# Setting unit 5 in a written order on all engines, with a table that places the six last conversions of w_out

## The chip, the core and the metric

The kernel runs on one core of one Trainium2 chip. The metric is the device time of one execution in microseconds (us). The engines are named as in the profile: PE (TensorE matmul), PEld (its weight load), DVE (VectorE), ACT (ScalarE), POOL (GpSimd), SP (SyncE, which issues most loads); "ACTq" and "SPq" are the sequencers of ACT and SP when they issue a DMA.

## The reference

Attention with a decaying state (8 heads, 4 batches, 768 positions, head size 64), then a feed-forward layer with a gate.

```python
for t in range(S):
    state = gamma[None, :, None, None] * state + np.einsum('bhd,bhe->bhde', k[:, :, t], v[:, :, t])
    y[:, :, t] = scale * np.einsum('bhd,bhde->bhe', q[:, :, t], state)
...
h = x @ w_in                       # 3072 x 512 by 512 x 2048
relu6 = np.clip(h + 3.0, 0.0, 6.0)
g = h * relu6 / 6.0
return (g @ w_out).astype(np.float32)   # 2048 x 512
```

The weights arrive as 64-bit floats.

## The kernel before, in words

**Tokens** are cut into 24 rows of 128 and 6 units of 512 (four rows each). A **tile of h** is 128 of the 2048 hidden columns by the 512 tokens of a unit, 16 tiles for a unit, 96 in all. Each is 12 matmuls of 128x128 by 128x512 (`products`, L431): both operands are split into a high and a low part, and three of the four products are taken for each of the four blocks of 128. `finish` then does the gate: `relu` on ACT (L438), `to_memory` (a DMA on the ACT queue, L465, that writes the tile *before* this one to the scratch tensor `gd`), and `times` on DVE (L442). Four PSUM buffers hold tiles of h.

**The first stage** (`head`) runs attention and units 0 and 1 in an order that is written out by hand. **`steady`** follows, a loop over `steps`: n = 0..15 are the tiles of unit 2, 16..31 of unit 3, 32..47 of unit 4, 48..63 of unit 5. At n = 1, 5, ... 45 it also does the attention of a row (`chunk_burst`): matmuls into `uz`, `sc` and `y`, ACT copies of the state out of `uz` (`keep`, L388), one DVE product (`weigh`, L352) and the split of the new x (L196, L199).

**Conversion of w_out.** It comes in 16 pieces (n_w2 = 0..15, two to each of eight tiles `w2c[j]`). One piece is `w2_steps`: a fetch into `st` (two buffers, 4 KB a partition each, issued on SP by `read`, L136), then steps with one letter each: `a` and `b` (DVE, L160, L164, bits of exponent and mantissa), `e` (ACT, L169), `q` and `f` (DVE, L172, L177, `f` being the last reader of `st`), `w` (DVE, L183), `1 2 3 0` (four DVE subtractions of 128x128, L116), `g` and `h` (ACT, L196, high parts), `k` and `l` (DVE, L199, low parts; `l` is the last reader of the buffer `ws`). The buffers `we`, `wb`, `ww` and `ws` exist once each. Pieces 0 to 9 are done in `steady`, four tiles of h for each piece, in the order `abqe`, `fw1`, `g230`, `hkl`.

**Who sets the order.** `head` and `steady` are under `manual_schedule` for PE, DVE, ACT and SP: their instructions keep the order in which the code names them. What is written outside goes through a planner that simulates the program, keeps a priority for each instruction, and may put an instruction between those of a set order. In the kernel before, `steady` ends at n = 47. Unit 5 is written outside it: PE alone has a set order there, and the planner places the gates of unit 5 and the conversions 10 to 15 (`build_w2`, called at tiles 4, 6, 8, 10, 12 and 14 of unit 5) on DVE, ACT and SP.

**The output stage** (L698) multiplies `gd` by `w2c` for three blocks of 1024 tokens, in four groups for each block, and each group in four rounds c = 0..3. A round loads `gd` into `gv` (two DMAs on SP, L668 in the first group), forms a sum on DVE (L119 in the first group), and splits two operands into `gc` (high part on ACT, L196; low part on DVE, L199). The first operand is split from `gv`, the second from the sum, which is kept in `spare`, a tile that takes over a slot of w_in after the last matmul that reads it. A round is 24 matmuls. The loads and sums of round 0 have high priority; the later DVE work of the first group is tied behind `end`, the last `times`:

```python
if sb == 0 and g == 0 and c == 0:
    first.enter_context(tc.high_priority())
elif sb == 0 and g == 0:
    first.enter_context(tc.issue_after(end))
```

`gv` rotates over three places: round 0 uses the pool `late` (in space that attention held), round 1 the pool `gv0`, round 2 the pool `gv1`, round 3 `late` again. `gv0` and `gv1` are laid over the space of the first stage, from its start, 8 KB a partition each; the pool that starts there is `wst`, with `st`, `we`, `wb`, `ww` and `ws` (16 KB in all).

Of the kernel before, what the change touches and what calls it, by code (L numbers as in the profile page):

```python
# [10 lines left out]
F32R = mybir.dt.float32r  # L11
# [9 lines left out]
P = 128  # L21
# [9 lines left out]
def retention_ffn(ctx: ExitStack, tc: tile.TileContext, qkv, w_in, w_out, dkc, dqc, dmc, tab, out, B, H, S, D):  # L31
# [8 lines left out]
    NF = w_in.shape[0]  # L40
# [3 lines left out]
    NROW = NT // P  # L44
    ROWS_B = S // P
    UR = 4
    UT = UR * P
    NU = NROW // UR
# [4 lines left out]
    FIRST = 3 * UR + 1  # L53
# [23 lines left out]
    BLK = 2 * P  # L77
    SLOT = 14 * BLK
    NSLOT = 10
    WHEN = (4, 6, 8, 10, 12, 14)  # L80
    STEADY = (NU - 1 - 2) * NF
    BUILT = 10
    PIECES = ("g230", "hkl", "abqe", "fw1")


    const = ctx.enter_context(tc.tile_pool(name="const", bufs=1))
    dram = ctx.enter_context(tc.tile_pool(name="dram", bufs=1, space=DRAM))
# [24 lines left out]
    def nm(s):  # L112
        return f"{s}_{next(serial)}"

    def dve_sub(out_, a, b):
        return nc.vector.tensor_tensor(out=out_, in0=a, in1=b, op=ALU.subtract)  # L116
# [29 lines left out]
    def fetch(src):  # L146
        st = wst.tile([P, src.shape[-1]], I64, tag="st", name=nm("st"), bufs=2)
        read(st, src)
        return st

    def conversion(st):

        n = st.shape[-1]
        words = st.bitcast(I32).rearrange("p (n w) -> p n w", w=2)
        lo, hi = words[:, :, 0], words[:, :, 1]
        t = {}

        def a():
            t["e"] = wst.tile([P, n], I32, tag="we", name=nm("we"))
            nc.vector.tensor_scalar(out=t["e"], in0=hi, scalar1=0x7FF00000, scalar2=None, op0=ALU.bitwise_and)  # L160

        def b():
            t["b"] = wst.tile([P, n], I32, tag="wb", name=nm("wb"))
            nc.vector.tensor_scalar(  # L164
                out=t["b"], in0=hi, scalar1=0xFFFFF, scalar2=0x100000, op0=ALU.bitwise_and, op1=ALU.bitwise_or
            )

        def e():
            nc.scalar.activation(out=t["e"], in_=t["e"], func=AF.Relu, scale=8.0, bias=ebias)  # L169

        def q():
            nc.vector.scalar_tensor_tensor(  # L172
                out=t["b"].bitcast(F32), in0=lo.bitcast(U32), scalar=2.0**-32, in1=t["b"], op0=ALU.mult, op1=ALU.add
            )

        def f():
            nc.vector.scalar_tensor_tensor(  # L177
                out=t["e"], in0=hi, scalar=-2147483648, in1=t["e"], op0=ALU.bitwise_and, op1=ALU.bitwise_or
            )

        def w():
            t["w"] = wst.tile([P, n], F32, tag="ww", name=nm("ww"))
            nc.vector.scalar_tensor_tensor(  # L183
                out=t["w"], in0=t["b"].bitcast(F32), scalar=2.0**-20, in1=t["e"].bitcast(F32), op0=ALU.mult, op1=ALU.mult
            )
            return t["w"]

        return {"a": a, "b": b, "e": e, "q": q, "f": f, "w": w}
# [6 lines left out]
    def high(hi, src):  # L195
        nc.scalar.activation(out=hi, in_=src, func=AF.Copy)  # L196

    def low(lo, hi, src):
        nc.vector.tensor_tensor(out=lo, in0=src, in1=hi, op=ALU.subtract)  # L199
# [8 lines left out]
    def place(shape, dtype, name, own):  # L208

        return wpool.tile(shape, dtype, tag="w0" if own else "w", name=name, bufs=1 if own else NSLOT - 1)  # L210
# [17 lines left out]
    w2c = {}  # L228

    def w2_steps(n, st):  # L230

        j, h = divmod(n, 2)
        if not h:
            w2c[j] = place([P, 7, 2, 2, P], F32R, nm("w2"), j == 5)
        made = conversion(st)
        to, t = w2c[j], {}

        def w():
            t["w"] = made["w"]().rearrange("p (b n) -> p b n", b=4)
            t["s"] = wst.tile([P, 4, P], F32, tag="ws", name=nm("ws"))  # L240

        def sub(o, a, b):
            block = lambda i: t["s"][:, i] if i < 4 else t["w"][:, i - 4]
            return lambda: dve_sub(block(o), block(a), block(b))

        steps = made | {
            "w": w,
            "1": sub(1, 4, 5),
            "2": sub(2, 7, 1),
            "3": sub(3, 7, 4),  # L250
            "0": sub(0, 2, 6),
            "g": lambda: high(to[:, 0:3, 0, h], t["w"][:, 1:4]),
            "h": lambda: high(to[:, 3:7, 0, h], t["s"]),
            "k": lambda: low(to[:, 0:3, 1, h], to[:, 0:3, 0, h], t["w"][:, 1:4]),
            "l": lambda: low(to[:, 3:7, 1, h], to[:, 3:7, 0, h], t["s"]),
        }
        return steps

    def build_w2(n):
        steps = w2_steps(n, fetch(w_out[divmod(n, 2)]))  # L260
        for k in "abeqfw1230gkhl":
            steps[k]()


    bits = place([TROWS, tab.shape[1]], I32, "bits", True)
    nc.scalar.dma_start(out=bits, in_=tab)
# [179 lines left out]
    def tile_of_h(u, jj):  # L446

        h = ps_h.tile([P, UT], F32, tag="h", name=nm("h"))
        for k in range(NK):
            products(h, u, jj, k)  # L450
        return u, jj, h

    def finish(u, jj, h):

        g, after = relu(h)
        to_memory(after)
        return times(u, jj, g, h)
# [103 lines left out]
    steps = [(u, jj) for u in range(2, NU) for jj in range(NF)]  # L561

    def steady():

        fetched, build, pending = [fetch(w_out[0, 0])], None, []
        load(FIRST)
        for n, step in enumerate(steps[:STEADY]):
            pending.append(tile_of_h(*step))
            for tile_ in pending[:-1]:
                finish(*tile_)  # L570
            del pending[:-1]
            b, row = (n - 2) // UR, FIRST + n // UR
            if n % UR == 2 and b < BUILT:
                build = w2_steps(b, fetched[b])
                if b + 1 < BUILT:
                    fetched.append(fetch(w_out[divmod(b + 1, 2)]))
            for k in PIECES[n % UR] if 0 <= b < BUILT else "":
                build[k]()
            if n % UR == 1:
                finish(*pending.pop())  # L580
                chunk_burst(row)
                if row + 1 < NROW:
                    load(row + 1)
        for tile_ in pending:
            finish(*tile_)

    engines = mybir.EngineType
    with tc.manual_schedule(engines={engines.PE, engines.DVE, engines.Activation, engines.SP}):
        head()
        steady()  # L590
    order = ExitStack()
    order.enter_context(tc.manual_schedule(engines={mybir.EngineType.PE}))

    att.close()
    late = ctx.enter_context(tc.tile_pool(name="late", bufs=1, side="right", reuse_waits="tile"))
    n_w2 = BUILT
    for u, jj in steps[STEADY:]:
        if jj in WHEN:
            build_w2(n_w2)
            n_w2 += 1  # L600
        end = finish(*tile_of_h(u, jj))
    to_memory(end)
    ph1.close()

# [43 lines left out]
    for sb in range(NT // TB):  # L648
        for g, ids in enumerate(GROUPS):
# [7 lines left out]
            for c in range(NFP // CP):  # L657
                with ExitStack() as first:
# [5 lines left out]
                    for jj in range(CP):  # L664
                        j = c * CP + jj
# [8 lines left out]
                    a, b = gv[:, 0], gv[:, 1]  # L674
                    s = sums[c]
# [17 lines left out]
                for i, gc in zip(ids, ops):  # L693
                    for h in range(2):
                        for jj in range(CP):
                            j = c * CP + jj
# [22 lines left out]
            else:  # L719
                for k, i, m in (("s", 2, 0), ("v", 3, 1)):  # L720
# [3 lines left out]
                    else:  # L724
                        for h in range(2):
                            for n in range(2 if (i, h) == (3, 1) else 1):
                                to = slice(n * BLK, (n + 1) * BLK) if (i, h) == (3, 1) else slice(0, UT)
# [88 lines left out]
```

## Time and profile before

| | |
|---|---|
| median of 3 runs | 579.49 us (578.61 to 583.13) |
| the profiled execution's own time | 581.04 us |
| its span, first to last instruction | 579.3 us |
| mean granted TensorE clock | 0.994 |
| PE busy | 565.8 us, 98% |
| DVE busy | 423.8 us, 73% |
| ACT busy | 247.1 us, 43% |
| POOL busy | 45.4 us, 8% |

A row of a timeline has the start in us, the duration in us, the engine, the line, the operation with output and input, the count, and in brackets the idle time just before with what ended it. A row of the chain of waits has start, length and what it was. A row of the stretches has, for each engine, busy time and in brackets the count, then the granted clock and the DMA share.

### The profile page before, as it was taken

What the parts mean: (1) busy time and instruction counts of PE and PEld (TensorE: products, weight loads), DVE (VectorE), ACT (ScalarE), POOL (GpSimd) and SP (SyncE); (2) the same over time, 40 slices, a digit from 0 to 9 for tenths busy, and PEclk for the clock granted to TensorE, in tenths of its full rate; (3) what the DMA queues carried; (4) which work ended last, traced back from release to release, by engine and by line L of the source; (5) the groups of instructions that cost most, each with busy time, mean ns of one, the idle gap of its engine ahead of it and who ended that gap; (6) DMA issues with size and microseconds to landing.
All of it is one profiled execution on the core that took longest, in us unless ns stands there. A gap on an engine that the chain in (4) does not pass through costs nothing.

```text
span 579.3 us, 12415 instructions
## 1 busy us (share of the span) xinstructions
PE 565.8 (98%) x5126; PEld 463.5 (80%) x5126; DVE 423.8 (73%) x588; ACT 247.1 (43%) x368; POOL 45.4 (8%) x51
## 2 busy tenths in 40 slices
PE   7799999999999999999999999999999999999997
PEld 5677887888888888888788888888888888888885
DVE  5489998733677678777726989679776698866871
ACT  3285544432444444434324555543434343344430
POOL 3201011121111111112000000000000000000000
PEclk9799999999999999999999999999999999999999
DMA  8866777835665666666542576465754757636611
GB/s 267 289 212 218 251 250 241 272 132 182 208 212 204 209 218 222 232 221 233 204 158 92 180 246 226 149 216 164 272 180 115 247 148 258 214 107 189 213 74 72
DMA packets 58324, 115.82 MB, mean 200 GB/s; under 512 B 5782, under 2 KB 6678, under 8 KB 58268
## 3 DMA queue, kind: packets, MB, share of 16 engines
q1 hardware_dynamic: 44144, 89.67, 48.1%
q10 hardware_dynamic: 14124, 25.37, 11.6%
q8 instruction: 40, 0.66, 0.5%
q14 instruction: 16, 0.13, 0.1%
HBM read 83.56 MB, written 31.46 MB: 199 GB/s over the span
## 4 chain that ended last, share of the span: by engine, by line
PE 92%; DMA 5%; issue 1%; DVE 1%; SPq 0%; POOL 0%; DVEq 0%
PE h L431 44%; PE o L698 40%; PE y L384 3%; PE sc L384 3%; PE uz L384 3%; DMA early<-in_qkv 2%; DMA st<-in_w_in 2%; DMA qt<-in_qkv 1%; SPq L136 0%; DVE we L160 0%; DVE wb L172 0%; DVE x L199 0%; POOL early L322 0%; DVE xr L525 0%; DVE we L177 0%
## 5 line engine op out<-in xcount | busy, mean ns | idle before, releaser
L431 PE MATMUL h<-x,w 128*128 128x512 f32 x1152 | 270.1, 393 | 0.4 <-ACT w L196 0.3
L431 PEld LDWEIGHTS h<-x,w 128*128 128x128 f32 x1152 | 214.0, 188 | 46.9 <-ACT w L196 0.7
L698 PE MATMUL o<-gc,w 128*128 128x512 f32 x1008 | 230.7, 391 | 0.0
L698 PEld LDWEIGHTS o<-gc,w 128*128 128x128 f32 x1008 | 189.2, 188 | 41.3
L438 ACT ACTIVATE g<-h,three 128x512 f32<-128x512 f32 x96 | 65.8, 687 | 104.2 <-PE h L431 97.6
L442 DVE SCALAR_TENSOR_TENSOR g<-g,h 128x512 f32<-128x512 f32 x96 | 65.5, 684 | 54.8 <-ACT g L438 54.7
L196 ACT ACTIVATE gc<-gv 128x1024 fp32r<-128x1024 f32 x48 | 50.9, 1060 | 63.1 <-PE o L698 56.4
L199 DVE TENSOR_TENSOR gc<-gv,gc 128x1024 fp32r<-128x1024 f32 x48 | 58.6, 1221 | 23.5 <-ACT gc L196 23.5
L196 ACT ACTIVATE gc<-spare 128x1024 fp32r<-128x1024 f32 x36 | 38.2, 1062 | 49.6 <-PE o L698 40.2
L199 DVE TENSOR_TENSOR gc<-spare,gc 128x1024 fp32r<-128x1024 f32 x36 | 43.9, 1221 | 10.3 <-ACT gc L196 10.3
L169 ACT ACTIVATE we<-we,ebias 128x512 int32<-128x512 int32 x32 | 23.0, 719 | 22.2 <-DVE we L160 22.2
L388 ACT ACTIVATE state<-uz 128x256 f32<-128x256 f32 x45 | 17.2, 382 | 29.8 <-PE y L384 16.0
L196 ACT ACTIVATE w<-ww 128x384 fp32r<-128x384 f32 (+2 forms) x34 | 18.6, 552 | 24.3 <-DVE ww L183 23.7
L183 DVE SCALAR_TENSOR_TENSOR ww<-wb,we 128x512 f32<-128x512 f32 x32 | 24.3, 760 | 0.9
L172 DVE SCALAR_TENSOR_TENSOR wb<-st,wb 128x512 f32<-128x512 uint32 x32 | 22.9, 717 | 0.8
L177 DVE SCALAR_TENSOR_TENSOR we<-st,we 128x512 int32<-128x512 int32 x32 | 23.1, 721 | 0.0
L316 POOL TENSOR_TENSOR qs<-qt,dq 128x512 f32<-128x512 f32 x16 | 22.3, 1394 | 3.3 <-DMA dq<-in_decays_q 3.3
L199 DVE TENSOR_TENSOR w<-ww,w 128x384 fp32r<-128x384 f32 (+2 forms) x34 | 20.0, 593 | 2.6 <-ACT w L196 2.5
L160 DVE TENSOR_SCALAR we<-st 128x512 int32<-128x512 int32 x32 | 13.5, 421 | 8.4 <-DMA st<-in_w_in 5.5
L116 DVE TENSOR_TENSOR spare<-spare,gv 128x1024 f32<-128x1024 f32 x12 | 14.7, 1222 | 5.7 <-DMA gv<-gd 5.7
L384 PE MATMUL y<-qs,state 64*64 64x64 f32 x480 | 18.3, 222 | 0.0
L384 PE MATMUL y<-am,vn 64*64 64x64 f32 x512 | 18.2, 219 | 0.0
(66 smaller groups left out, 427.6 us busy)
## 6 DMA issues: line engine op xcount, KB each, us to landing
gd<-g ACTq DMA_DIRECT2D x96, 256.0 KB, 3.0
gv<-gd SPq DMA_DIRECT2D x48, 512.0 KB, 4.8
gv<-gd SPq DMA_DIRECT2D x48, 256.0 KB, 3.1
st<-in_w_in SPq DMA_DIRECT2D x16, 512.0 KB, 4.4
st<-in_w_out SPq DMA_DIRECT2D x16, 512.0 KB, 4.8
early<-in_qkv SPq DMA_DIRECT2D x28, 256.0 KB, 4.3
kt<-in_qkv SPq DMA_DIRECT2D x16, 256.0 KB, 3.4
qt<-in_qkv SPq DMA_DIRECT2D x16, 256.0 KB, 4.1
```

Source lines behind the costliest of these rows:

```text
L169: nc.scalar.activation(out=t["e"], in_=t["e"], func=AF.Relu, scale=8.0, bias=ebias)
L172: nc.vector.scalar_tensor_tensor(out=t["b"].bitcast(F32), in0=lo.bitcast(U32), scalar=2.0**-32, in1=t["b"], op0=ALU.mult, op1=ALU.add)
L177: nc.vector.scalar_tensor_tensor(out=t["e"], in0=hi, scalar=-2147483648, in1=t["e"], op0=ALU.bitwise_and, op1=ALU.bitwise_or)
L183: nc.vector.scalar_tensor_tensor(out=t["w"], in0=t["b"].bitcast(F32), scalar=2.0**-20, in1=t["e"].bitcast(F32), op0=ALU.mult, op1=ALU.mult)
L196: nc.scalar.activation(out=hi, in_=src, func=AF.Copy)
L199: nc.vector.tensor_tensor(out=lo, in0=src, in1=hi, op=ALU.subtract)
L316: nc.gpsimd.tensor_tensor(out=t["qs"], in0=t["qt"], in1=d, op=ALU.mult)
L384: nc.tensor.matmul(out_, lhs, rhs, start=start, stop=True, skip_group_check=True)
L431: nc.tensor.matmul(h, t[:, o, a], xs[u][b][:, k], start=k + n == 0, stop=(k, n) == (NK - 1, 2), skip_group_check=True)
L438: return g, nc.scalar.activation(out=g, in_=h, func=AF.Relu, bias=three).ins
L442: ins = nc.vector.scalar_tensor_tensor(out=g, in0=g, scalar=6.0, in1=h, op0=ALU.min, op1=ALU.mult)
L698: nc.tensor.matmul(acc[i][h] if last else acc[i][:, h], w2c[j][:, RIGHT[i], x, h], gc[:, y, jj], start=j == 0 and n == 0, stop=j == NFP - ...
```

## The change

`steady` runs through all 64 steps, so unit 5 has a set order on PE, DVE, ACT and SP as well; it returns the last `times` as `end`. The table `PLAN` names for each n which letters of which piece follow the tile of h and the gate of the tile before it. For pieces 0 to 9 it gives the order that `PIECES` gave. Pieces 10 to 15 are cut finer: piece 10 starts at n = 42 and ends at 52, piece 15 starts at n = 60 and ends at 63. `FETCH` names the n at which a piece is fetched. `w2c[j]` is allocated when it is first written. The pool `late` is opened after `steady`.

```diff
-    WHEN = (4, 6, 8, 10, 12, 14)
-    STEADY = (NU - 1 - 2) * NF
-    BUILT = 10
-    PIECES = ("g230", "hkl", "abqe", "fw1")
+    STEADY = 10
+    PLAN = {UR * b + 2 + i: f"{b}{k}" for b in range(STEADY) for i, k in enumerate(("abqe", "fw1", "g230", "hkl"))}
+    PLAN |= {
+        42: "10abqe", 43: "10fw1", 44: "10230", 46: "11abqe", 47: "11f", 52: "10gkhl 11w1", 53: "11g230 12abqe",
+        54: "12f 11hkl", 55: "12w1230g 13ae", 56: "12hkl 13bq", 57: "13fw1 14a", 58: "13g230 14ebq", 59: "14f 13hkl",
+        60: "14w1230g 15ae", 61: "14hkl 15bq", 62: "15fw12g", 63: "1530hkl",
+    }
+    FETCH = {UR * b + 2: b + 1 for b in range(STEADY + 1)} | {47: 12, 48: 13, 55: 14, 58: 15}
...
-        if not h:
-            w2c[j] = place([P, 7, 2, 2, P], F32R, nm("w2"), j == 5)
...
+        def to(y, b):
+            if j not in w2c:
+                w2c[j] = place([P, 7, 2, 2, P], F32R, nm("w2"), j == 5)
+            return w2c[j][:, b, y, h]
...
-        fetched, build, pending = [fetch(w_out[0, 0])], None, []
+        builds, pending = {0: w2_steps(0, fetch(w_out[0, 0]))}, []
         load(FIRST)
-        for n, step in enumerate(steps[:STEADY]):
+        for n, step in enumerate(steps):
             pending.append(tile_of_h(*step))
             for tile_ in pending[:-1]:
                 finish(*tile_)
             del pending[:-1]
...
+            if n in FETCH:
+                b = FETCH[n]
+                builds[b] = w2_steps(b, fetch(w_out[divmod(b, 2)]))
+            for word in PLAN.get(n, "").split():
+                d = 2 if word[:2].isdigit() and int(word[:2]) >= STEADY else 1
+                for k in word[d:]:
+                    builds[int(word[:d])][k]()
+            row = FIRST + n // UR
+            if n % UR == 1 and row <= NROW:
                 finish(*pending.pop())
                 chunk_burst(row)
                 if row + 1 < NROW:
                     load(row + 1)
...
+        return finish(*pending.pop())
...
-    for u, jj in steps[STEADY:]:
-        if jj in WHEN:
-            build_w2(n_w2)
-            n_w2 += 1
-        end = finish(*tile_of_h(u, jj))
     to_memory(end)
```

More of the change, by code (lines that the diff above doesn't have):

```diff
@@ L232, in w2_steps @@
         j, h = divmod(n, 2)
-        if not h:
-            w2c[j] = place([P, 7, 2, 2, P], F32R, nm("w2"), j == 5)
-        made = conversion(st)
-        to, t = w2c[j], {}
+        made, t = conversion(st), {}
+        def to(y, b):
+            if j not in w2c:
+                w2c[j] = place([P, 7, 2, 2, P], F32R, nm("w2"), j == 5)
+            return w2c[j][:, b, y, h]
         def w():
@@ L251, in w2_steps @@
             "0": sub(0, 2, 6),
[L252 to L255, printed above, removed]
-        }
-        return steps
[L259 to L262, printed above, removed]
+            "g": lambda: high(to(0, slice(0, 3)), t["w"][:, 1:4]),
+            "h": lambda: high(to(0, slice(3, 7)), t["s"]),
+            "k": lambda: low(to(1, slice(0, 3)), to(0, slice(0, 3)), t["w"][:, 1:4]),
+            "l": lambda: low(to(1, slice(3, 7)), to(0, slice(3, 7)), t["s"]),
+        }
+        return steps
     bits = place([TROWS, tab.shape[1]], I32, "bits", True)
@@ L571, in steady @@
             del pending[:-1]
[L572 to L579, printed above, removed]
+            if n in FETCH:
[7 more added lines that the diff above has]
+            if n % UR == 1 and row <= NROW:
                 finish(*pending.pop())
@@ L583, in steady @@
                     load(row + 1)
-        for tile_ in pending:
-            finish(*tile_)
+        return finish(*pending.pop())
     engines = mybir.EngineType
@@ L589, in retention_ffn @@
         head()
-        steady()
+        end = steady()
     order = ExitStack()
@@ L595, in retention_ffn @@
     late = ctx.enter_context(tc.tile_pool(name="late", bufs=1, side="right", reuse_waits="tile"))
-    n_w2 = BUILT
-    for u, jj in steps[STEADY:]:
-        if jj in WHEN:
-            build_w2(n_w2)
-            n_w2 += 1
-        end = finish(*tile_of_h(u, jj))
     to_memory(end)
```

## The prediction

> **What bounds the kernel now.** I read the page's first part, then the busy time by stretches around the edited tiles, then the chain of waits.
>
> ```profile
> span 579.3 us, 12415 instructions
> ...
> PE 565.8 (98%) x5126; PEld 463.5 (80%) x5126; DVE 423.8 (73%) x588; ACT 247.1 (43%) x368; POOL 45.4 (8%) x51
> ```
>
> ```profile
> core 0: us, PE busy (x) PEld busy (x) DVE busy (x) ACT busy (x) POOL busy (x), PEclk, DMA share, GB/s
> 216.00:280.00 64.00, 64.00 (x779) 52.80 (x781) 48.50 (x85) 27.76 (x49) 11.36 (x10) 1.00 0.67 227
> 280.00:296.00 16.00, 14.85 (x213) 12.39 (x205) 10.09 (x20) 5.25 (x10) 0.00 (x0) 1.00 0.45 158
> 296.00:345.20 49.20, 49.20 (x217) 40.75 (x218) 36.67 (x74) 23.27 (x36) 0.00 (x0) 1.00 0.49 167
> ```
>
> ```profile
> 280.98 1.15 issue
> 282.13 0.27 PE uz L384 x2
> ...
> 295.98 49.19 PE h L431 x216
> 345.17 230.53 PE o L698 x1008
> ```
>
> PE is the bound. In the stretch 296 to 345.2, which holds the last two tiles of unit 4 and all of unit 5, PE is busy for all of 49.20 us at clock 1.00; DVE (36.67) and ACT (23.27) have room. The chain runs over one unbroken piece of 216 matmuls into 1008 matmuls of the output stage, with no step between. So the stage that is rewritten has nothing to give. The one loss near the edit is earlier: 1.15 us of "issue" in the attention burst of n = 41, and PE is busy for 14.85 of 16.00 us there, the same 1.15.
>
> The chain does not name the cause. The timelines do, of SP, of DVE and of ACT:
>
> ```profile
> 272.23 0.33 SPq L136 DMA_DIRECT2D st<-in_w_out  x1
> ```
>
> ```profile
> 277.42 0.43 DVE L160 TENSOR_SCALAR we<-st 128x512 int32<-128x512 int32 x1 [2.69 <-DMA st<-in_w_out]
> 277.76 0.42 DVE L164 TENSOR_SCALAR wb<-st 128x512 int32<-128x512 int32 x1
> 278.10 0.68 DVE L442 SCALAR_TENSOR_TENSOR g<-g,h 128x512 f32<-128x512 f32 x1
> ...
> 280.51 0.68 DVE L442 SCALAR_TENSOR_TENSOR g<-g,h 128x512 f32<-128x512 f32 x1
> ```
>
> ```profile
> 281.22 0.33 ACTq L465 DMA_DIRECT2D gd<-g  x1
> 281.64 0.38 ACT L388 ACTIVATE state<-uz 128x256 f32<-128x256 f32 x1 [1.02 <-DVE w L199]
> ```
>
> Piece 10 isn't in the set order of unit 4, yet its fetch went out at 272.23 and its step a stands on DVE between gates of tiles 38 and 39: the planner put it there. The data came 5.2 us after the issue, and DVE stood for 2.69 us with the gate of tile 39 queued behind. The gate of tile 40 ended at 281.19, ACT's store of that tile went out at 281.22, the copy of the state behind it began at 281.64 and ended at 282.02, and PE's next write to uz, which must wait for that copy, started at 282.13. So the bracket on the last row (a DVE low part) isn't the whole of it: the store behind the late gate held ACT.
>
> **The change, part by part.** Durations are those of the profiled execution (581.04 us: span 579.3, 1.74 around it). It lies 1.55 above the median of the runs; I work out the difference and set it on the median.
>
> *Pieces 0 to 9, the fetches, the allocation on first use.* Letters and n are the same for pieces 0 to 9. The fetch of 10 moves into the set order at n = 38; on SP it stands behind the same loads as the one at 272.23, so that it is issued then again. Fetches 11 to 15 are issued when step f of the piece two before lets go of `st`. The tightest is 15: it needs f of 13 (n = 57), and its a comes three tiles later, 8.2 us at 49.19/18 = 2.73 us a tile, against 5.2 us for the landing above. Cost 0 under that cover; if a landing took 3 us more, DVE would wait with times behind it, and four PSUM buffers would still keep PE fed for two tiles. I take 0.
>
> *Piece 10 goes to n = 42.* Its a then stands behind the burst of n = 41, and its data have landed at 277.4, some five us before. Nothing queued ahead of the gates 39 and 40 waits for a DMA. Gate 40 falls back to where ACT's relu of tile 40 allows it, some 4 us earlier (2.69 of waiting and a, b, q, f of piece 10, at least 0.34 each). What is late next is nothing that PE waits for: in the stretch 216 to 280, with five bursts, PE is busy for all of 64.00 us. **-1.15 us**; bounds 0 (some other floated instruction takes the place) and -1.15 (PE cannot be more than busy).
>
> *The load of the tiles 52 to 63.* The steps' spacing is read off the last conversion of the kernel before:
>
> ```profile
> 334.46 0.68 DVE L172 SCALAR_TENSOR_TENSOR wb<-st,wb 128x512 f32<-128x512 uint32 x1
> 335.06 0.68 DVE L442 SCALAR_TENSOR_TENSOR g<-g,h 128x512 f32<-128x512 f32 x1
> 335.66 0.68 DVE L177 SCALAR_TENSOR_TENSOR we<-st,we 128x512 int32<-128x512 int32 x1
> 336.38 0.69 DVE L183 SCALAR_TENSOR_TENSOR ww<-wb,we 128x512 f32<-128x512 f32 x1
> 337.10 0.49 DVE L116 TENSOR_TENSOR ws<-ww 128x128 f32<-128x128 f32 x2
> ...
> 337.77 0.69 DVE L442 SCALAR_TENSOR_TENSOR g<-g,h 128x512 f32<-128x512 f32 x1
> 338.37 0.28 DVE L116 TENSOR_TENSOR ws<-ws,ww 128x128 f32<-128x128 f32 x1
> 338.58 0.55 DVE L199 TENSOR_TENSOR w<-ww,w 128x384 fp32r<-128x384 f32 x1
> 339.36 0.69 DVE L199 TENSOR_TENSOR w<-ws,w 128x512 fp32r<-128x512 f32 x1 [0.23 <-ACT w L196]
> 339.97 1.22 DVE L119 TENSOR_TENSOR spare<-gv 128x1024 f32<-128x1024 f32 x1
> 341.10 0.68 DVE L442 SCALAR_TENSOR_TENSOR g<-g,h 128x512 f32<-128x512 f32 x1
> ```
>
> From start to next start: q 0.60, times 0.60, f 0.72, w 0.72, a subtraction 0.21, k 0.55, l 0.61, the sum of round 0 1.13, and as much for a low part of 1024, which lasts the same 1.22; a and b 0.34 from the rows at 277. The fullest tile of the table is n = 56 or 61: times 0.60 + k 0.55 + l 0.61 + b 0.34 + q 0.60 = 2.70, of 2.73. No tile overruns by itself, so the gates hold and unit 5 itself costs 0. But nothing is spare from 52 on, and the sum and the low part of round 0 (2.26 us) must go between; DVE is behind by about that at the end.
>
> *The passage to the output stage.* This is where the change can cost. The rows are SP's, ACT's, DVE's, and the landing of the `gv` loads between 290 and 375:
>
> ```profile
> 296.07 1.36 SPq L668 DMA_DIRECT2D gv<-gd  x2
> 336.37 1.19 SPq L668 DMA_DIRECT2D gv<-gd  x2
> 340.08 1.21 SPq L668 DMA_DIRECT2D gv<-gd  x2
> ```
>
> ```profile
> 301.96 1.06 ACT L196 ACTIVATE gc<-gv 128x1024 fp32r<-128x1024 f32 x1 [2.31 <-DMA gv<-gd]
> ```
>
> ```profile
> 345.93 0.69 DVE L442 SCALAR_TENSOR_TENSOR g<-g,h 128x512 f32<-128x512 f32 x1 [1.79 <-ACT g L438]
> 346.53 1.22 DVE L119 TENSOR_TENSOR spare<-gv 128x1024 f32<-128x1024 f32 x1
> 347.67 1.22 DVE L199 TENSOR_TENSOR gc<-gv,gc 128x1024 fp32r<-128x1024 f32 x1
> ```
>
> ```profile
> DMA to landing us min/median/max: 2.8/4.4/8.3
> ```
>
> Round 0's first operand is split at 302, far ahead, among the set gates of tiles 46 and 47. That shows the high-priority work passing set instructions, and I expect it again. Round 1's loads go out at 336.37, right at the end of f of piece 15 (335.66 + 0.68 = 336.34), and round 2's at 340.08, at the end of its l (339.36 + 0.69 = 340.05): `gv0` lies over the two `st`, `gv1` over `we` to `ws`. So the table's later end delays these loads.
>
> New times, on the clock of before. Times of tile 60 starts at 337.77; n = 61 takes 2.70 to 340.47; the sum of round 0 goes between, 341.60; times of 61, 342.20; f of 15 ends at 342.9. Round 1's pair goes out then, 6.5 us later than before. Landing of a pair: 5.9 us by the rows at 296.07 and 301.96; bounds 5.0 (second issue 0.6 behind, median 4.4) and 8.9 (0.6 + 8.3, a load with five others around it). I take 5.9, the same two loads at a like DMA share: 348.8. DVE by then: w, 1 and 2, round 0's low part, times, 3 and 0, k, l (347.4), times of 63 (348.0). So round 1's sum starts at 348.8, its first low part at 349.9, and that ends at 351.15. PE reaches round 1 after 24 matmuls of 230.53/1008 = 0.229 us, 345.17 + 5.49 = 350.66, and needs the low part one matmul later, 350.89. **+0.3 us**; bounds 0 (landing 5.0) and 3.2 (8.9). By the Trainium skill, "DMA: Bandwidth & Descriptors", section on the anatomy of one DMA, a transfer takes about 2.0 us and its bytes at 436 GB/s; as an estimate 4.4 us for this pair's 1 MB, and then nothing would be lost here and the sum would be -1.15. The row of 5.9 speaks against it, and I go by the row.
>
> Round 2: l of 15 ends at 347.4, the pair lands at 353.3, sum and low part end at 355.7, PE needs them at 356.4. Costs 0, with 0.7 to spare. The rest is off PE's path: the output stage gives DVE 5.49 us for 3.4 us of work in a round, so it catches up.
>
> Sum: -1.15 + 0.3 = -0.85; 580.2 by the profiled execution, **578.6 on the median**.
>
> **The rivals.** *The loads of round 1 land late (slower).* Price: each us of landing beyond 5.6 us after 342.9 is a us of PE idle. It outweighs the 1.15 from a landing of 6.8 us on. At 8.9 the gap is 3.2, and the time 579.5 - 1.15 + 3.2 = 581.6. For it: the 8.3 in the row, and no margin on DVE. Against it: that 8.3 fell among six `gv` loads within 8 us, where here the pair is first and alone with the stores.
>
> *Round 0 waits for the set order to end.* If the planner doesn't let its work pass the last set instructions, the sum and low part follow times of tile 63, with the sum at 346.5 as round 1's is in the rows of before, since DVE isn't held up by them: 346.5 + 1.13 + 1.22 = 348.85 against 345.4 needed, a gap of 3.45, and the time 581.8. Against it: the rows at 277.42 and 301.96, both between set instructions. The Trainium skill, "TensorE: Matmul & The Clock Gate", Part 1, says that PE's clock falls to half after an idle window of about 3.4 us; at the gap of 1.15 the granted clock stayed 1.00, and no stretch here shows a gap that long. By that rule such a gap would cost an estimated 1.7 us more.
>
> *Nothing is removed.* Other work that the planner floats (round 0's splits, which stood ACT for 2.31 us) takes the place ahead of a burst. Then 579.5 + 0.3 = 579.8. Against it: the space of round 0's loads comes free only after the last burst.
>
> **How the numbers follow.** Forecast 0.57 (578.6), late loads 0.20 (up to 581.6), nothing removed 0.16 (579.8), round 0 late 0.07 (581.8). The runs of before spread by 4.5 us, and 1% is 5.8 us, about what a measurement of this kernel can tell from no change; no case reaches that. Range: from 577.2, the lowest run of before less 1.15 and a little, to 581.8, which takes in the late loads and leaves out the top of the last case. Faster by over 1% 0.03, within 0.93, slower 0.04.
>
> **What would show it.** Right: no step of "issue" near 281 in the chain; a of piece 10 after the burst of n = 41, without a DMA wait; PE busy throughout unit 5; round 1's loads issued near 341.8 (342.9 less the 1.15), and at most a short PE gap near 349.7, where round 1 starts. Wrong: PE gaps inside unit 5 (a gate behind a fetch), a gap at the first output matmul (round 0 late) or one of 1 us or more at round 1 or 2, or DVE waiting for `st` in the tiles 52 to 60. The forecast fails most easily on the landing time of the two loads and on the order that the planner gives the sums of rounds 1 and 2 on DVE: a sum of round 2 put ahead of the second low part of round 1 would hold that back until 353.3 and cost some 1.7 us.

## The result, and the profile after

The changed kernel takes **586.04 us** (median of 12 runs, 584.17 to 588.3) where the kernel before takes 580.38 (12 runs beside it, 578.58 to 583.34). The ratio is **1.0088, 95% interval 1.0065 to 1.0111**, or 5.1 us (3.8 to 6.4); the quotient of the two medians, 1.0098 or 5.7 us, lies inside it. The forecast of 578.6 us and its range up to 581.8 are both wrong, and so is the sign.

The page of the kernel after, first part:

```profile
span 584.8 us, 12412 instructions
...
PE 567.0 (97%) x5126; PEld 463.4 (79%) x5126; DVE 423.0 (72%) x588; ACT 246.8 (42%) x368; POOL 46.3 (8%) x51
```

The work is the same; the span is 5.5 us longer. The stretches of the kernel after show where:

```profile
core 0: us, PE busy (x) PEld busy (x) DVE busy (x) ACT busy (x) POOL busy (x), PEclk, DMA share, GB/s
280.00:296.00 16.00, 16.00 (x241) 13.47 (x234) 8.73 (x17) 5.83 (x10) 0.00 (x0) 1.00 0.33 120
296.00:345.20 49.20, 49.20 (x219) 40.70 (x218) 35.77 (x71) 21.15 (x33) 0.00 (x0) 1.00 0.46 156
345.20:375.00 29.80, 25.35 (x103) 20.18 (x102) 24.09 (x27) 15.79 (x17) 0.00 (x0) 0.94 0.60 199
...
354.60:358.00 3.40, 3.38 (x8) 2.71 (x9) 2.44 (x3) 1.07 (x2) 0.00 (x0) 0.50 1.03 392
```

The 1.15 us loss of PE in 280 to 296 is gone, and PE is busy throughout unit 5, as forecast. The loss is all in the first 30 us of the output stage: PE is idle for 4.45 us, and then runs at half its clock for 3.4 us. PE's timeline and its waits in the kernel after name the place:

```profile
344.70 4.97 PE L691 MATMUL o<-gc,w 128*128 128x512 f32 x21
353.27 0.49 PE L691 MATMUL o<-gc,w 128*128 128x512 f32 x1 [3.60 <-ACT gc L199]
354.62 11.66 PE L691 MATMUL o<-gc,w 128*128 128x512 f32 x43 [0.85 <-DVE gc L202]
```

This is the passage from round 0 to round 1. The chain of waits of the kernel after gives the account (rows of it from unit 5 on, with the steps of DVE between left out):

```profile
294.97 43.76 PE h L430 x192
...
354.62 226.62 PE o L691 x983
```

The 216 matmuls that precede the output stage take 49.2 us without a break, as before, so that the first output matmul (S from here on) starts at 294.97 + 49.20 = 344.17, against 345.17 before: -1.00. From S to the 26th matmul pass 10.45 us instead of 25 x 0.229 = 5.72: +4.73, which is 4.45 of idle time and 0.28 for the lone matmul of 0.49. The other 983 take 226.62 instead of 224.81 at that pace: +1.81, the half clock. Together +5.54, the difference of the two spans.

What PE waited for is in the timelines of SP, ACT and DVE (kernel after):

```profile
340.05 1.19 SPq L661 DMA_DIRECT2D gv<-gd  x2
...
345.07 1.18 SPq L661 DMA_DIRECT2D gv<-gd  x2
...
349.45 1.17 SPq L661 DMA_DIRECT2D gv<-gd  x2
```

```profile
337.05 0.72 ACT L172 ACTIVATE we<-we,ebias 128x512 int32<-128x512 int32 x1 [0.87 <-DVE we L163]
...
337.68 0.67 ACT L437 ACTIVATE g<-h,three 128x512 f32<-128x512 f32 x1
...
352.16 1.06 ACT L199 ACTIVATE gc<-gv 128x1024 fp32r<-128x1024 f32 x1 [1.35 <-DMA gv<-gd]
```

```profile
336.60 0.42 DVE L163 TENSOR_SCALAR we<-st 128x512 int32<-128x512 int32 x1
338.75 1.23 DVE L122 TENSOR_TENSOR spare<-gv 128x1024 f32<-128x1024 f32 x1 [1.74 <-PE h L430]
339.90 0.68 DVE L441 SCALAR_TENSOR_TENSOR g<-g,h 128x512 f32<-128x512 f32 x1
...
341.57 1.22 DVE L202 TENSOR_TENSOR gc<-spare,gc 128x1024 fp32r<-128x1024 f32 x1
...
344.36 0.69 DVE L180 SCALAR_TENSOR_TENSOR we<-st,we 128x512 int32<-128x512 int32 x1
...
349.34 0.68 DVE L441 SCALAR_TENSOR_TENSOR g<-g,h 128x512 f32<-128x512 f32 x1
349.94 1.22 DVE L122 TENSOR_TENSOR spare<-gv 128x1024 f32<-128x1024 f32 x1
351.07 1.22 DVE L202 TENSOR_TENSOR gc<-gv,gc 128x1024 fp32r<-128x1024 f32 x1
352.21 1.22 DVE L122 TENSOR_TENSOR spare<-gv 128x1024 f32<-128x1024 f32 x1
353.34 1.22 DVE L202 TENSOR_TENSOR gc<-gv,gc 128x1024 fp32r<-128x1024 f32 x1
```

Step f of piece 15 (L180) ends at 345.05, that is S + 0.9, and lets go of the space in which round 1's pair of loads lands. The pair goes out at 345.07 (second row of SP), and ACT gets its data at 352.16, 7.1 us later. The pair at 340.05 is round 3's (it reads the last two tensors of `gd`): the planner put it ahead. On DVE too, the sum and low part at 349.94 and 351.07 are round 3's, and those at 352.21 and 353.34 round 1's. So three things come late together: f of 15, the landing, and DVE, which has no idle time from 349.34 to 354.56. Of the three the landing binds: ACT's high part needs the data and ends at 353.22, DVE's low part needs the high part, and it starts at 353.34.

A second passage is late as well, and the first one hides it. Step l of 15 ends at 349.42 and lets go of the space of round 2's pair; the pair goes out at 349.45 (third row of SP), ACT gets its data at 356.72, and DVE's low part of it runs from 357.88 to 359.10. Without the gap at round 1, PE would have needed it at S + 49 x 0.229 = 355.4, 3.7 us earlier.

### The profile page after: what moved, and what is told of

Same layout as the page of the kernel before. It is cut to its first block, busy times and chain, and to the rows that moved or that the text cites. A ratio compares the mean times of both kernels' runs of the same rounds, so it can differ in the third digit from the quotient of the medians.

```text
span 584.8 us, 12412 instructions
## 1 busy us (share of the span) xinstructions
PE 567.0 (97%) x5126; PEld 463.4 (79%) x5126; DVE 423.0 (72%) x588; ACT 246.8 (42%) x368; POOL 46.3 (8%) x51
## 4 chain that ended last, share of the span: by engine, by line
PE 84%; DVE 8%; DMA 5%; issue 2%; SPq 0%; ACT 0%; POOL 0%; DVEq 0%; ACTq 0%
PE o L691 39%; PE h L430 37%; DMA st<-in_w_in 3%; PE y L383 3%; PE uz L383 2%; PE sc L383 2%; DMA early<-in_qkv 2%; DVE g L441 2%; DVE we L180 1%; DVE w L202 1%; DVE wb L175 1%; DVE gc L202 1%; DVE ww L186 1%; DVE wb L167 1%; SPq L139 0%
## 5 line engine op out<-in xcount | busy, mean ns | idle before, releaser
L180 DVE SCALAR_TENSOR_TENSOR we<-st,we 128x512 int32<-128x512 int32 x32 | 21.9, 683 | 0.0
L122 DVE TENSOR_TENSOR spare<-gv 128x1024 f32<-128x1024 f32 x12 | 14.7, 1223 | 7.7 <-DMA gv<-gd 5.9
L119 DVE TENSOR_TENSOR gv<-gv 128x1024 f32<-128x1024 f32 x12 | 14.7, 1223 | 5.1 <-DMA gv<-gd 4.8
```

What stands on the lines that cost most here:

```text
L180: nc.vector.scalar_tensor_tensor(out=t["e"], in0=hi, scalar=-2147483648, in1=t["e"], op0=ALU.bitwise_and, op1=ALU.bitwise_or)
```

## The experiments

"Before" in each is the kernel before, run beside it on the same chip; the chip and the time of before differ between experiments, so compare ratios. Where intervals overlap, what tells two kernels apart is the idle time in their profiles. Line numbers shift by a few from kernel to kernel; the operation tells which is meant. The summary, with f of 15's end counted from S, and PE's idle time from unit 5 to round 2:

| kernel | f of 15 ends | PE idle | clock after | ratio to before |
|---|---|---|---|---|
| after | S + 0.9 | 4.45 | 0.50 | 1.0088 [1.0065, 1.0111] |
| early, twice | S - 8.8 | 0 | 1.00 | 0.9981 [0.9955, 1.0007], 0.9986 [0.9958, 1.0014] |
| fill | as after | 1.40, and 3.37 filled | 1.00 | 1.0056 [1.0032, 1.0081] |
| moved | as after, not waited for | 2.52 | 1.00 | 1.0062 [1.0033, 1.0091] |
| sumlate | S - 0.6 | 5.89 | 0.50 | 1.0137 [1.0102, 1.0171] |
| behind | S + 0.9 | 4.70 | 0.50 | 1.0125 [1.0091, 1.0160] |
| sum_behind | S - 0.6 | 2.70 | 1.00 | 1.0062 [1.0039, 1.0086] |
| loadlate | not in question | 5.17 | 0.50 | 1.0129 [1.0096, 1.0162] |
| packed | S - 1.9 | 5.45, of it 1.69 in unit 5 | 1.00 | 1.0090 [1.0064, 1.0116] |
| copy | S - 8.8 | 0 | 1.00 | 0.9982 [0.9956, 1.0009] |
| e_later | S - 2.0 | 1.40 | 1.00 | 1.0001 [0.9979, 1.0023] |
| both | S - 0.6, not waited for | 1.56 | 1.00 | 1.0007 [0.9980, 1.0033] |

### early: pieces 10 and 11 started in unit 4, unit 5 left to the planner

```diff
-        for n, step in enumerate(steps):
+        for n, step in enumerate(steps[:48]):
...
+    for u, jj in steps[48:]:
+        if jj in (4, 6, 8, 10, 12, 14):
+            b = 8 + jj // 2
+            if b not in builds:
+                builds[b] = w2_steps(b, fetch(w_out[divmod(b, 2)]))
+            for k in {10: "gkhl", 11: "w1230gkhl"}.get(b, "abeqfw1230gkhl"):
+                builds[b][k]()
+        end = finish(*tile_of_h(u, jj))
```

> One part alone: pieces 10 and 11 begin in the set order of unit 4 as in the changed kernel, and unit 5 with the rest of the conversions is left to the planner as in the kernel before. Theory: the PE gap of 1.15 us in the burst of n = 41 goes and nothing else changes; 1.0 to 1.4 us under the kernel before (ratio 0.998). Rival (the gap had another cause, or the planner floats other work into its place): same time as the kernel before.

Measured 578.64 us against 579.01. The chain of waits of this kernel has neither the step of "issue" near 281 nor a break at the passage:

```profile
293.81 49.19 PE h L430 x216
343.00 230.53 PE o L700 x1008
```

> The same kernel as the one with pieces 10 and 11 started in unit 4 and unit 5 left to the planner, timed in five rounds once more to narrow its interval: 0.9981 [0.9955, 1.0007] before. If the 1.15 us gap of PE is all that it takes away, 0.997 to 0.999 again, with the upper end below 1.

Measured 579.32 against 579.63. The half of the change that lies in unit 4 is worth some 1.3 us by its profile: in the chains of waits, the blocks of 48 matmuls of h on either side of the burst start at 267.51 and 280.70 here, 13.19 us apart, and at 268.32 and 282.82 before, 14.50 apart. The two timings agree with that in sign and size; but neither interval excludes no change, and the upper end below 1 that the second was to give was not reached.

### fill: 14 matmuls that nobody uses, between rounds 0 and 1

```diff
+                if sb == 0 and g == 0 and c == 0:
+                    fill = ps_o[1].tile([P, 2, UT], F32, tag="o0", name=nm("fill"))
+                    for _ in range(14):
+                        nc.tensor.matmul(fill[:, 0], w2c[0][:, RIGHT[4], 0, 0], ops[0][:, 0, 0], start=True, stop=True, skip_group_check=True)
```

> The changed kernel with 14 matmuls between rounds 0 and 1 of the output stage, whose product is not used; they keep PE at work through most of the gap of 3.60 and 0.85 us. Theory (the clock's share): the 1.7 to 2.0 us that the output stage loses beyond the gap come from a granted clock of 0.50 in the 3.4 us after it. Then the clock stays 1.00 there, the gap's end stays near 354.6, and the time is 1.7 to 2.0 us under the changed kernel, some 3.6 to 3.9 over the kernel before. Rival (the matmuls after the gap are slow because loads are landing at 390 GB/s at that time): no change, 5.5 over the kernel before.

Measured 583.18 against 579.01. PE is kept at work, and the clock doesn't fall (stretch of this kernel behind the passage, and the last row of its chain of waits):

```profile
354.00:358.00 4.00, 2.60 (x11) 1.86 (x11) 3.13 (x3) 1.68 (x2) 0.00 (x0) 1.00 1.01 389
```

```profile
355.98 225.37 PE o L691 x983
```

The 983 matmuls take 1.25 us less than after, although the loads land at 389 GB/s there as they did after (392), so the rival is out. The 0.56 that is left over 224.81 lies, as far as the rows show, around round 2, whose low part isn't done until 361.65. By time, +3.2 us over before instead of +5.1; the two intervals overlap, so it is the clock column that shows it, not the time alone.

### moved: round 1's loads laid over space that is free long before

```diff
-        for n in ("gv0", "gv1", "gc2", "v", "p", "gc0", "gc1", "q")
+        for n in ("gc0", "gv1", "gc2", "v", "p", "gv0", "gc1", "q")
```

> The changed kernel with the pools gv0 and gc0 in each other's place, so that round 1's loads no longer wait for the last reader of st; they then lie over x of unit 4. Theory A (late loads make the gap): round 1's loads leave right behind round 3's pair, near 341.2 instead of 345.07, and land by 348; the gap shrinks to what DVE leaves, since its last gate ends at 350.0: sum and low part end at 352.3, needed at 349.9, a gap of 2.4 with no fall of the clock; 1.0 to 2.0 us over the kernel before. Rival B (DVE's lateness alone makes the gap, the loads do not matter): gap still 4.4 and the time 5.5 over the kernel before.

Measured 583.2 against 579.01. PE's waits in this kernel:

```profile
PE o L691 <- DVE gc L202: 1.9, 2, 1.5
PE o L691 <- ACT gc L199: 0.7, 1, 0.7
```

Without any wait for `st`, 2.52 us of the 4.45 stay. At round 1 it is 2.17: DVE's last gate is as late as after, and the sum and low part of round 1 can't come before it. The other 0.35 is at round 2, where the chain of waits runs through the landing of round 2's pair. The size is as expected. The time, +3.6 us (1.9 to 5.3), is more than the 1.4 that this gap less 1.15 makes. By the profile, S to the end of the last matmul is 3.3 us longer than before, since the matmul ahead of each wait also lasts longer (0.50 us against 0.229); less the gain of unit 4 (1.0 to 1.4) that makes 1.9 to 2.3, just inside the interval.

### sumlate: round 0's sum tied behind gate 61

```diff
+                    if sb == 0 and g == 0 and c == 0:
+                        with tc.issue_after(gates[61]):
+                            dve_add(s, a, b)
```

> The changed kernel with the sum of round 0 tied on DVE behind the gate of tile 61, so that it no longer stands ahead of the gate of tile 60 waiting for PE (1.74 us of DVE's time). Theory A: f of piece 15 ends some 2 us earlier (343 instead of 345.04), round 1's loads leave and land 2 us earlier, DVE is some 2 us less behind, and the gap falls from 4.45 to about 2.5 without a fall of the clock; 1.5 to 2.5 us over the kernel before. Rival C (DVE is late because the table fills each tile, not because of that wait): f of 15 and the gap stay, 5.5 over.

Measured 587.51: a miss. f of 15 does end earlier (S - 0.6 instead of S + 0.9), but the planner lets round 3's pair go first on SP, at 339.92, and round 1's follows at 341.3. It lands last (timeline of DVE in this kernel):

```profile
350.85 1.23 DVE L122 TENSOR_TENSOR spare<-gv 128x1024 f32<-128x1024 f32 x1 [1.87 <-DMA gv<-gd]
```

That is 9.5 us behind its issue. The gain on f was lost to a landing among six loads. The clock fell early and stayed down (stretches of this kernel; PE had gone idle at 346.57):

```profile
350.00:354.00 4.00, 1.53 (x3) 0.93 (x4) 3.15 (x3) 2.11 (x2) 0.00 (x0) 0.50 0.91 352
354.00:358.00 4.00, 4.00 (x11) 3.13 (x10) 4.00 (x5) 2.12 (x2) 0.00 (x0) 0.50 0.45 145
```

### behind: the loads of rounds 2 and 3 tied behind round 1's

```diff
+                        if sb == 0 and g == 0 and c >= 2:
+                            with tc.issue_after(loads[c - 1]):
+                                loads[c] = nc.sync.dma_start(out=gv[:, :, jj], in_=gd[j][:, :, t0 + UT : t0 + TB]).ins
```

> The changed kernel with the loads of rounds 2 and 3 tied on SP behind those of round 1, so that round 3's pair no longer goes first. Times from S, the first output matmul. Theory D (round 3's pair, which goes out ahead, takes the DMA engines from round 1's): round 1's pair still leaves at S + 0.9, behind f of piece 15, but lands after 5.9 instead of 7.0, at S + 6.8; DVE also does round 1 ahead of round 3; the low part ends at S + 9.2, needed at S + 5.7, a gap of 3.5 instead of 4.45; 2.5 over the kernel before if the clock stays up, 4.2 if it falls. Rival A (only the late step f counts): landing still 7.0, gap 4.4, 5.1 over.

Measured 587.16: a miss too. The pair is first and alone among loads, and it doesn't land sooner (SP, then DVE, then the landing of this pair's two loads, each from its own issue):

```profile
345.32 1.18 SPq L665 DMA_DIRECT2D gv<-gd  x2
```

```profile
353.00 1.22 DVE L122 TENSOR_TENSOR spare<-gv 128x1024 f32<-128x1024 f32 x1 [2.74 <-DMA gv<-gd]
```

```profile
DMA to landing us min/median/max: 7.0/7.0/7.0
```

So round 3's pair ahead isn't what made the landing long; why a pair alone takes 7.0 here and 5.9 in the next kernel stays open.

### sum_behind: both ties

> Both edits, the sum of round 0 behind the gate of tile 61 and round 1's loads ahead of the others. With the sum's edit alone f of piece 15 ended at S - 0.6, but round 1's pair went out behind round 3's and landed at S + 9.7. Theory D: round 1's pair now leaves at S - 0.5 and, alone, lands at S + 5.4; DVE's last gate ends at S + 4.8; the low part ends at S + 7.8, a gap of 2.1, no fall of the clock; 1.0 to 1.5 over the kernel before, against some 8 over with the sum's edit alone. Rival (landing is late for another reason than the neighbours): it lands at S + 8 or later, 5 or more over.

Measured 582.29 against 578.93. PE's waits:

```profile
PE o L701 <- ACT gc L199: 1.6, 1, 1.6
PE o L701 <- DVE gc L202: 1.1, 2, 0.8
```

2.7 us in all (2.44 at round 1, 0.26 at round 2), at clock 1.00; 2.1 were expected. f of 15 ends 1.5 us earlier against S than after, the pair goes out at 343.42, and DVE still waits 1.27 us for it. Gate 60 no longer stands behind the sum, but now it waits for its relu (DVE):

```profile
338.23 0.69 DVE L441 SCALAR_TENSOR_TENSOR g<-g,h 128x512 f32<-128x512 f32 x1 [1.36 <-ACT g L437]
```

### loadlate: early, with round 1's loads made late and nothing else

```diff
-        for n in ("gv0", "gv1", "gc2", "v", "p", "gc0", "gc1", "q")
+        for n in ("gc2", "gv1", "gv0", "v", "p", "gc0", "gc1", "q")
```

In this kernel (early otherwise) the loads of round 1 lie over the x of unit 5, which is free only after the last tile of h (`gc2` takes the old place of `gv0`).

> The suspected cost by itself, without unit 5's set order: the kernel with the early part alone, and with gv0 moved over x of unit 5, which is read until the last tile of h. DVE, ACT and the conversions stay as the planner has them; only round 1's loads leave late, at S. Theory (the landing of round 1's loads is on PE's path by itself): they land at S + 4.4 to 5.9, sum and low part end 2.4 later, against S + 5.7 needed: a gap of 1.1 to 2.6, and 0.1 to 1.5 over the kernel before, 1.2 to 2.6 over the early part alone. Rival B (DVE's lateness makes the gap, the loads have slack): no gap, 1.0 under the kernel before.

Measured 587.36, more than expected. PE's waits, and ACT at the end of them:

```profile
PE o L700 <- ACT gc L199: 4.7, 1, 4.7
PE o L700 <- DVE gc L202: 0.5, 1, 0.5
```

```profile
351.80 1.06 ACT L199 ACTIVATE gc<-gv 128x1024 fp32r<-128x1024 f32 x1 [2.40 <-DMA gv<-gd]
```

The pair went out at 342.8, at S, with four loads ahead of it, and landed 9.0 us later. The conversions end early here, so a late landing alone is enough for a gap of 5 us.

### packed: a denser table

Each of the pieces 12 to 15 is spread over three tiles, the last ending at n = 61 instead of 63; the subtractions of 11 to 15 go to POOL; both ties of sum_behind.

```diff
...
+        54: "12qfw1230", 55: "12gkhl 13abe", 56: "13qfw1230", 57: "13gkhl 14abe", 58: "14qfw1230", 59: "14gkhl 15abe",
+        60: "15qfw1230", 61: "15gkhl",
...
+            eng = nc.gpsimd if n > STEADY else nc.vector
```

> Unit 5 in a set order on all engines with the causes removed: a denser table that ends piece 15 at n = 61, with its f at n = 60, the four subtractions of pieces 11 to 15 on POOL instead of DVE, the sum of round 0 behind the gate of tile 61, and round 1's loads ahead of rounds 2 and 3. Theory (the order itself costs nothing, the late end of the table does): f of 15 ends near S - 6, round 1's pair lands by S, no PE gap at round 1; 1.0 to 1.4 under the kernel before, like the early part alone. Rival (a set order makes DVE and ACT wait for each other and for PE, whatever the table): a gap of 1 us or more in unit 5 or at the passage; at or over the kernel before.

Measured 585.39: a miss. The four subtractions take POOL about 2.2 us for a piece, ACT's high part waits for them, DVE's low part for ACT, and the gate behind that low part holds PE inside unit 5:

```profile
341.91 3.02 PE L431 MATMUL h<-x,w 128*128 128x512 f32 x12 [1.69 <-DVE g L442]
...
350.35 0.49 PE L702 MATMUL o<-gc,w 128*128 128x512 f32 x1 [2.65 <-ACT gc L199]
```

The second row stands in the middle of round 0: its sum is tied behind gate 61, which ends at 348.07 here, 3.1 us behind S, so that 3.42 us of the idle time are round 0's. It shows that a set order can turn one engine's lateness into another's, but not whether a set order costs by itself. The next kernel tells that.

### copy: unit 5 in a set order, with the order that the planner chose in early

```diff
+    LAST = """
+        10g 10h 10k 10l r51 11w t51 11g 11132 11k 110 r52 11h 12a 12b 12e t52 12q 11l 12f F14 12w r53 t53
+        ...
+        15f 15w 15132 r60 t60 15g 150 15h 15k 15l r61 t61 r62 t62
+    """
```

r and t are relu and times of a tile, F a fetch, a number and letters a piece's steps; piece 15 is done before gate 61.

> Unit 5 keeps a set order on all four engines, but with other contents: instruction by instruction the order that stands in the trace of the kernel whose unit 5 was left to the planner (no PE gap, 0.9981 of the time before), so that piece 15's last low part stands ahead of gate 61 and not behind gate 63; round 0's sum is tied behind gate 61 and rounds 2 and 3 behind round 1's loads. Theory (the place that the table gives the last pieces is what costs): f of 15 ends 7 to 9 us ahead of the first output matmul, round 1's pair lands in time, PE has no gap over 0.5 us at the passage, and the time is 0.5 to 1.5 us below that of before (ratio 0.997 to 0.999). Rival (a set order on ACT and DVE costs by itself, since an engine waits behind another's instruction that a planned order would have let pass): a gap of 1 us or more somewhere in unit 5 or at the passage, and a time at or above that of before.

Measured **578.22** against 579.63. Chain of waits and SP's issue of round 1's pair:

```profile
292.53 49.19 PE h L434 x216
341.72 230.53 PE o L722 x1008
```

```profile
332.92 1.19 SPq L688 DMA_DIRECT2D gv<-gd  x2
```

No gap, and the pair goes out 8.8 us ahead of S, as in the kernel before (336.37). So a set order for unit 5 on all engines need not cost anything (the upper end of the interval is 1.0009), and the places in the table of the change do. This kernel changes all the places at once and has both ties, so it doesn't single out one of them.

### e_later: sum_behind, with the exponent step of pieces 12, 13 and 15 a tile later

```diff
...
-        60: "14w1230g 15ae", 61: "14hkl 15bq", 62: "15fw12g", 63: "1530hkl",
+        60: "14w1230g 15a", 61: "15e 14hkl 15bq", 62: "15fw12g", 63: "1530hkl",
```

> The changed kernel's table with round 0's sum tied behind gate 61 and rounds 2 and 3 behind round 1's loads (which gave a gap of 2.7 us and 1.0062), and now the exponent step e of pieces 12, 13 and 15 a tile later, so that the relu of the tile is not held on ACT until DVE has reached that piece's step a. Theory (ACT's order holds the gates): gates wait for ACT 1 to 2 us less in 312 to 350, f of 15 ends 1 to 1.5 us earlier against the first output matmul, round 1's pair lands as much earlier, and the gap of PE falls from 2.7 to about 1.5 us: time 0.5 to 1.5 us less than 582.3. Rival (DVE's own 31 us of work in the table sets the end, and ACT only takes up its slack): f of 15 and the gap as they were, 2.5 to 3 us.

Measured 580.36 against 579.63: 0.7 us over before, where sum_behind was 3.4 over (582.29 against 578.93), and their intervals lie apart. ACT in e_later, at the place of the rows at 337.05 above, and PE's waits:

```profile
334.90 0.69 ACT L437 ACTIVATE g<-h,three 128x512 f32<-128x512 f32 x1
334.90 0.33 ACTq L464 DMA_DIRECT2D gd<-g  x1
335.62 0.72 ACT L172 ACTIVATE we<-we,ebias 128x512 int32<-128x512 int32 x1
```

```profile
PE o L701 <- DVE gc L202: 1.4, 2, 0.8
```

The relu goes ahead of e; DVE's gates wait for ACT for 0.9 us in 312 to 352, against 5.1 in sum_behind. f of 15 ends at S - 2.0, 1.4 us earlier than in sum_behind, and 1.3 us of the gap are gone (0.81 is left at round 1, 0.59 at round 2). So these 1.4 us were the order of the steps and not DVE's own work; of ACT's order by these waits, though the edit also puts f of 12 behind the low part of 11.

### both: round 1's landing and the planner's order taken away together

The pools of moved and the two ties of sum_behind.

> The changed kernel's table with three things taken away together: round 1's loads lie over a buffer that is free long before (as in the kernel with the two exchanged), round 0's sum is tied behind gate 61, and rounds 2 and 3 are tied behind round 1's loads. If landing and DVE's late last gate are the two causes and there is no third, what is left is DVE alone: last gate at 348 to 349 by the profile, the sum and the first low part of round 1 behind it, a gap of 0.8 to 1.7 us at the passage, clock 1.00, and a time 0 to 1.5 us over that of before. If the landing was the whole cause, no gap and 1 us below before; if something else of the table costs, a gap of 2 us or more.

Measured 579.51 against 579.63. PE's waits:

```profile
PE o L701 <- DVE gc L202: 1.6, 2, 1.4
```

DVE's last gate ends at 346.26, 4.8 us behind S, and sum and low part of round 1 follow at once: 1.35 us, with round 1's landing and the planner's order gone. The other 0.21 is at round 2, and the chain of waits goes there:

```profile
346.26 5.81 DMA gv<-gd
352.15 1.23 DVE spare L122
353.38 1.15 DVE gc L202
354.57 219.60 PE o L701 x959
```

This is round 2's pair, which waits for l of 15 and goes out at 345.69. Even with round 1 in time, PE would have stood until 354.57 there. So DVE's lateness and round 2's late pair each cost about as much, one over the other, and the two together eat the gain of unit 4.

## Why the prediction was wrong

**Right: the gain.** Piece 10 moved behind the burst, PE is busy for 16.00 of 16.00 us there, and from the block of h ahead of the burst to the one behind it pass 13.14 us (268.67 to 281.81) instead of 14.50: 1.36, a little more than the 1.15 that was forecast as the most. S is only 1.00 earlier because this execution was 0.35 later up to there. S by itself is a poor sign: in the profiled executions of kernels that are the same up to unit 5 it lies between 341.1 and 345.4. **Right: unit 5 without a PE gap**, although DVE's gates did slip; four PSUM buffers covered that. Round 0 was in time, so that rival (0.07) is out. "Nothing is removed" (0.16) is out as well.

**Wrong: the passage, +0.3 forecast, 4.73 measured.** The rule of the forecast was good: "each us of landing beyond 5.6 us after 342.9" is a us of PE idle. Round 1's pair was to land at S + 3.6 and landed at S + 8.0, 4.4 later; 0.3 + 4.4 = 4.7, against 4.45 of idle time. In sum_behind (data at S + 6.0) the same rule gives 2.7, and 2.44 was measured at round 1; in e_later (S + 4.4) 1.1, and 0.81; in behind (S + 8.6) 5.3, and 4.70: always a little too much. What failed is what went into it:

1. *"f of 15 ends at 342.9"* (S - 2.3). It ended at S + 0.9, 3.2 us later. The sum took it that "no tile overruns by itself, so the gates hold", from DVE's 2.70 of 2.73 us. Two waits were left out. The sum of round 0 was put "between", as work; the planner put it ahead of gate 60, where it stood 1.74 us for the matmul that still read its slot (DVE row at 338.75). And ACT counted as free: e of 15 stands there ahead of the tile's relu and must wait for a, which DVE reaches at the end of its words, so that the gate of that tile waits for ACT, which waits for DVE (ACT rows at 337.05 and 337.68). The low part of round 0, which the forecast had behind f, stood ahead of it too (1.13 us, DVE row at 341.57). The tie of the sum gave back 1.5 us (sum_behind): it took away the 1.74 and put that low part behind f, but then gate 60 waited 1.36 for its relu. The later e gave back 1.4 more (e_later): 2.9 of the 3.2 in all.
2. *"Landing of a pair: 5.9 us."* It took 7.1, inside the bounds of 5.0 to 8.9 but with no margin left for it. The 5.9 was round 0's pair; in the kernel before, round 1's own pair (out at 336.37) took up to 6.7, with single loads between 4.7 and 6.1 us. The argument against a long landing, that the pair "is first and alone with the stores", fell twice: it wasn't first (after, sumlate), and alone it took 7.7 from first issue to use (behind). The 5.9 lay nearer than the estimate of 4.4 for 1 MB by the Trainium skill, "DMA: Bandwidth & Descriptors", section on the anatomy of one DMA, whose fit is for one transfer that GpSimd issues, where these are two that SP issues; both were too short.
3. *DVE through with the last gate at 348.0, S + 2.8.* Its last gate ended at 350.0, S + 5.9, and round 3's sum and low part came before round 1's, the reordering that the prediction's last sentence feared of round 2. In the changed kernel the later landing covers this; with round 1's landing taken away, 2.17 us stay at round 1 (moved), or 1.35 with the ties (both).
4. *The clock.* The forecast priced the late loads at the idle time alone. After waits of 3.60 and 0.85 us the matmuls cost 1.81 more (983 of them, 226.62 for 224.81), with the granted clock at 0.50 for 3.4 us. The prediction named the rule, of the Trainium skill, "TensorE: Matmul & The Clock Gate", Part 1, and its estimated 1.7 us, but only beside another rival whose gap it put at 3.45. The changed kernel's trace agrees with its price (1.81), and it belonged to every case with a gap of that size.
5. *Round 2: "Costs 0, with 0.7 to spare."* l of 15 ended at S + 5.2 instead of S + 2.2, and the pair took 7.3 us instead of 5.9. The changed kernel hides it behind the gap of round 1, but it sets the end in sum_behind, moved, e_later and both, and would have cost some 3.7 us by itself.

The rival that came true is "the loads of round 1 land late" (0.20), beyond its own price: its end was put at 581.6, with 3.2 us of gap, no clock, and f of 15 where the forecast had it. Each late term had been worked out from the forecast's favourable value of the others, while steps f and l, the landings behind them and DVE's last gates all hang on the last piece, placed at n = 60 to 63. The kernel copy, with a set order but the last piece before gate 61, has no gap; and loadlate, where only round 1's landing is late, has one of 5.17 us. How much each of the other places in the table adds isn't shown, apart from e.

## What to carry to other kernels

When work is moved late into a stage that is full, count the margin at the next passage, not the load of the stage: here the last reader of a buffer moved from 8.8 us before the next stage to 0.9 us behind its start, and the load over that buffer takes some 6 to 9.5 us until its data are used. Count it for the passages behind the next one too: here round 2 was late as well, and shortening the gap at round 1 only brought that to light. In a written order, check for each instruction that waits what stands behind it on its own engine, the "free" engine too: an exponent step of 0.7 us ahead of a relu held the gates. To settle whether an order or its contents cost, write out the good order by hand and run it.

## What the runs showed of the hardware that I had not expected

In four kernels the granted clock fell to 0.50, with idle times of PE of 3.60 (and 0.85 more), 4.18, 4.66 and 5.37 us; it stayed 1.00 in those with 2.65 and less, and 14 matmuls in the gap prevented the fall. The Trainium skill, "TensorE: Matmul & The Clock Gate", Part 1, puts the idle window at about 3.4 us, and this split agrees with it. But the fall isn't tied to 3.4 us of idle time: in sumlate it came near 348.9, 2.3 us after PE went idle, and in loadlate near 350.5, also after about 2.2. Nor does it always last the 3.4 us of the changed kernel: in behind the clock stood at 0.50 from 353.2 to 360.0, in sumlate to 359.1, some 10 us; the 983 matmuls took 227.17 and 227.77 us there. What decides between these lengths is not shown.

The same pair of loads (512 KB each) took 5.1 and 6.5 us from issue to landing in the kernel after, 5.9 in sum_behind, 5.8 in e_later, 7.0 in behind, and 7.5 to 8.9 in sumlate with others ahead of it. Company alone doesn't order these: in both, with one load of `st` 0.4 us ahead and no other load of `gv` in flight, it took 7.4 to 8.5. I could not place the spread.
